# Which engine adds the second convolution tap of the first groups, and which queue stores y of group 3

## The chip, the cores and the metric

The kernel runs on one core of a Trainium2 chip. The metric is the device time of one execution in microseconds (us), as the median of several runs. TensorE is called PE here, VectorE DVE, ScalarE ACT, GpSimd POOL and SyncE SP, as the profile calls them.

## The reference

The input `x` has shape (8, 4224, 192). A causal depthwise convolution with 7 taps comes first: the 192 channels are 8 heads of 24 channels, each head has one softmaxed set of 7 weights, and each output position is the weighted sum of itself and the 6 positions ahead of it. A layer norm and a two-layer MLP (192 to 768 to 192, ReLU) are added to the result.

```python
w = softmax(weight)                       # (8 heads, 7 taps)
y = sum_k w[h, k] * x_padded[s + k]       # per head of 24 channels
xn = (y - mean(y)) / sqrt(var(y) + 1e-6) * g_ln
out = y + relu(xn @ w_ch1) @ w_ch2
```

## The kernel before

**Groups.** Each batch row of 4224 positions is laid on 128 partitions of 33 neighbouring positions. The work is cut into 18 groups of n positions per partition: batch 0 gives groups 0 to 3 with n = 6, 7, 8 and 12, each other batch gives one of 16 and one of 17. In words, a group goes through these steps:

- `load_x(g)` brings x to the tile `xg` (two buffers), issued on SP.
- The convolution makes `y` (two buffers). `first_tap` is 8 ACT multiplies (L336), one per head. `second_tap` is 8 ACT multiplies into a tile `tb` (one buffer, L349), and two DMAs on the POOL queue that add `tb` onto `y` in SBUF (L352); they are called the accumulating DMAs here. `conv(g, k0, k1)` adds taps k0 to k1 - 1 on DVE, 8 instructions per tap (L363).
- `transpose` (L374, DVE) makes `yt` for PE. `store_y` (L431) stores y to the output; later `add_to_out` (L631, POOL queue) adds the MLP's result onto these rows in HBM. `moments` (L389) and `root` are the layer norm's statistics on DVE.
- `up(g)` is the first matrix product on PE (L473); ACT applies the ReLU into `ht` (L485).
- The second product is `down(g)` (L509) for groups 0 to 2, whose results ACT copies out in `park` (L613) and DVE transposes in `finish` (L656). From group 3 on it is `down_fast(g)`: seven half products (`product`, matmuls L553, ACT copies L558) of the Strassen kind, with sums of halves of `ht` on DVE between them (`half_sum`, L531). For group 17 a part of it is done by `down`.

**Order.** The schedule is manual: each engine works through its instructions in the order in which the program issues them, and semaphores do the rest. The loop turns over the groups; in the turn of group g, PE does the products of group g, while DVE finishes the convolution of group g + 1 and ACT starts that of group g + 2. PE has no other work that it could turn to.

In the turn of groups 0 to 2 the taps for g + 2 stand after the ReLUs and ahead of `down`:

```python
conv(g + 1, 2 if g else 1)
transpose(g + 1)
store_y(g + 1)
...
first_tap(g + 2)
second_tap(g + 2)
down(g)
park(g)
```

From group 3 on the 16 tap steps for group g + 2 (8 of `first_tap`, then 8 of `second_tap`) are handed out by `some_taps` in between the half products of `down_fast(g)`; after each of the first four come `many` of them, 3 where n is 16 or 17 and 2 in group 3.

In the turn of group 3 DVE has in order: taps 2 to 4 of group 4, the first three half sums (1,0), taps 5 and 6, the transpose, and inside `down_fast(3)` nine half sum instructions: three for (1,1), three for (0,0), three for (0,1). The fifth half product reads (1,1), the sixth (0,0), the seventh (0,1).

Of the kernel before, what the change touches and what calls it, by code (L numbers as in the profile page):

```python
# [16 lines left out]
def kernel(  # L17
# [27 lines left out]
    nc = tc.nc  # L45
# [10 lines left out]
    J = 17  # L56
# [268 lines left out]
    def first_tap(g, on_act=True, heads=(0, H)):  # L325
        n = groups[g][2]
        if g == 1:

            y[g] = y[0][:, groups[0][2] :]
        elif heads[0] == 0:  # L330
            y[g] = ypool.tile([P, J, D], F32, tag="y", name=f"y{g}")
        for h in range(*heads):
            cs = slice(h * GRP, h * GRP + GRP)
            dst, src, tap = y[g][:, 0:n, cs], xg[g][:, 0:n, cs], taps[:, h, 0:1]
            if on_act:
                nc.scalar.mul(dst, src, tap)  # L336
            else:
                nc.vector.tensor_scalar(out=dst, in0=src, scalar1=tap, scalar2=None, op0=ALU.mult)
# [3 lines left out]
    def second_tap(g, heads=(0, H)):  # L342

        n = groups[g][2]
        if heads[0] == 0:
            tb[g] = bpool.tile([P, J, D], F32, tag="tb", name=f"tb{g}")
        for h in range(*heads):
            cs = slice(h * GRP, h * GRP + GRP)
            nc.scalar.mul(tb[g][:, 0:n, cs], xg[g][:, 1 : 1 + n, cs], taps[:, h, 1:2])  # L349
        if heads[1] == H:  # L350
            for j1, j2 in ((0, n // 2), (n // 2, n)):
                nc.gpsimd.dma_start(  # L352
                    out=y[g][:, j1:j2].rearrange("p j d -> p (j d)"),
                    in_=tb[g][:, j1:j2].rearrange("p j d -> p (j d)"), accum_op=ALU.add,
                )

    def conv(g, k0=1, k1=K, heads=H):
        n = groups[g][2]
        t = xg[g]
        for k in range(k0, k1):  # L360
            for h in range(heads):
                cs = slice(h * GRP, h * GRP + GRP)
                nc.vector.scalar_tensor_tensor(  # L363
                    out=y[g][:, 0:n, cs], in0=t[:, k : k + n, cs], scalar=taps[:, h, k : k + 1],
                    in1=y[g][:, 0:n, cs], op0=ALU.mult, op1=ALU.add,
                )

    def transpose(g):
        n = groups[g][2]
        if g == 1:  # L370
            yt[g] = yt[g - 1][:, groups[0][2] :]
        else:
            yt[g] = tpool.tile([P, J, NC, C], F32, tag="yt", name=f"yt{g}")
        nc.vector.transpose(  # L374
            yt[g][:, 0:n].rearrange("p j c t -> p (j c t)"),
            y[g][:, 0:n].rearrange("p j d -> p (j d)"),
        )
# [3 lines left out]
    def moments(g):  # L381

        n = groups[g][2]
        if g % 2:
            sums[g] = sums[g - 1][:, groups[g - 1][2] :]
        else:
            sums[g] = spool.tile([P, 2 * J, nc.vector.BN_STATS_DIM], F32, tag="st", name=f"st{g}")
        for j in range(n):
            nc.vector.bn_stats(out=sums[g][:, j, :], in_=y[g][:, j, :])  # L389
# [36 lines left out]
        rstd[g] = rt  # L426
        rstd[g + 1] = rt[:, groups[g][2] :]

    def store_y(g):
        b, j0, n = groups[g]  # L430
        nc.sync.dma_start(  # L431
            out=outr[b, :, j0 * D : (j0 + n) * D], in_=y[g][:, 0:n].rearrange("p j d -> p (j d)")
        )

# [93 lines left out]
    def half_sum(g, dst, left, right, op):  # L528
        a = ht[g][0]
        for f in range(FC):  # L530
            nc.vector.tensor_tensor(  # L531
                a[:, *dst, f], a[:, *left, f], a[:, *right, f], op=op
            )

    def down_fast(g):
        n = fast[g]
        w = n * T
        a = ht[g][0]
        cs = cpool.tile([P, NC, NFAST * C], F32, tag="cs", name=f"cs{g}")[:, :, 0 : n * C]
        cs = cs.rearrange("p c (j h t) -> p c j h t", h=2, t=T)  # L540
        part = cpool.tile([P, 3, CH, NFAST * T], F32, tag="part", name=f"part{g}")[:, :, :, 0:w]
        part = part.rearrange("p v c (j t) -> p v c j t", t=T)
        banks = [
            psum.tile([P, 512], F32, tag="ps", name=f"pd{g}_{c}_{i}")
            for c in range(CH) for i in range(2)
        ]

        def product(bank, left, right, to, first):
            for c in range(CH):
                dst = banks[2 * c + bank]  # L550
                for f in range(FC):
                    for q in range(NQ):
                        nc.tensor.matmul(  # L553
                            dst[C * q : C * q + C, 0:w], right[:, f, C * c : C * c + C],
                            left[:, f, q], start=(first and f == 0), stop=(f == FC - 1),
                            skip_group_check=True,
                        )
                nc.scalar.copy(  # L558
                    to[:, c], dst[:, 0:w].rearrange("p (j t) -> p j t", t=T)
                )  # L560

        b = [w2[:, e * FC : e * FC + FC, d * (D // 2) : (d + 1) * (D // 2)]
             for e in range(2) for d in range(2)]
        c11, c21 = cs[:, 0:CH, :, 0], cs[:, 0:CH, :, 1]
        c12, c22 = cs[:, CH:NC, :, 0], cs[:, CH:NC, :, 1]
        todo = [(tap, h) for tap in (first_tap, second_tap) for h in range(H)] if g + 2 < NG else []

        def some_taps(times):
            for tap, h in todo[:times]:
                tap(g + 2, heads=(h, h + 1))  # L570
            del todo[:times]

        many = 3 if n >= J - 1 else 2
        product(0, a[:, 0, 0], b[0], c11, True)
        some_taps(many)
        product(1, a[:, 1, 0], w2sums[:, 2], c22, True)
        some_taps(many)
        product(1, a[:, 1, 1], w2sums[:, 3], part[:, 1], False)
        some_taps(many)
        product(1, a[:, 0, 1], b[2], part[:, 0], True)  # L580
        some_taps(many)
        half_sum(g, (1, 1), (1, 1), (1, 0), ALU.subtract)
        half_sum(g, (0, 0), (1, 1), (0, 0), ALU.add)
        half_sum(g, (0, 1), (0, 1), (1, 1), ALU.subtract)
        nc.vector.tensor_tensor(c11, c11, part[:, 0], op=ALU.add)
        product(0, a[:, 1, 1], w2sums[:, 1], c21, False)
        if g + 1 == NG:
            finish_fast(g, 0, cs, part)
        some_taps(2)
        product(0, a[:, 0, 0], w2sums[:, 0], part[:, 2], False)  # L590
        some_taps(2)
        product(0, a[:, 0, 1], b[3], c12, False)
        some_taps(len(todo))
        return cs, part

    def finish_fast(g, half, cs, part):
        n = fast[g]
        ot = ots[g] if half else out_tile(g)
        fresh = cs[:, CH * half : CH * half + CH, :, 1]
        nc.vector.tensor_tensor(fresh, fresh, part[:, 1 + half], op=ALU.add)  # L600
        for c in range(CH * half, CH * half + CH):
            nc.vector.transpose(  # L602
                ot[:, 0:n, C * c : C * c + C], cs[:, c].rearrange("p j h t -> p j (h t)")
            )
# [73 lines left out]
    for g in range(NG):  # L678
        if g + 2 < NG:
            load_x(g + 2)  # L680
        up(g)
        last = g + 1 == NG
        if not fast[g]:

            conv(g + 1, 2 if g else 1)
            transpose(g + 1)
            store_y(g + 1)
            if g < 2:
                moments(g)
            first_tap(g + 2)  # L690
            second_tap(g + 2)
            down(g)
            park(g)
            if g == 1:
                finish(0)
                root(0)
                w2_sums()
                moments(2)
                finish(1)
            elif g == 2:  # L700
                moments(3)
                root(2)
                finish(2)
            continue
        if not last:
            conv(g + 1, 2, 5)
        half_sum(g, (1, 0), (0, 0), (1, 0), ALU.subtract)
        if not last:
            conv(g + 1, 5, K)
            transpose(g + 1)  # L710
            if g + 2 < NG:
                store_y(g + 1)
        parts = down_fast(g)
        if not last:

            moments(g + 1)
            if g % 2 == 0:
                root(g)
        for half in range(last, 2):
            finish_fast(g, half, *parts)  # L720
        if last:
            add_and_store(g, slice(0, fast[g]))
            down(g)
            finish(g)
# [30 lines left out]
```

## Time and profile before

| | |
|---|---|
| median of 4 runs | 1015.29 us (1014.51 to 1015.6) |
| the profiled execution | 1015.57 us, of which its span is 1013.8 us |
| PE busy | 997.0 us, 98% of the span |
| DVE, ACT, POOL busy | 838.7, 567.3, 64.7 us |
| DMA queue q0 (issued by POOL), q1 (by SP and ACT) | 26.2% and 16.4% of 16 engines' span |
| granted PE clock, mean | 0.998 |

The rows that the prediction reads give the start of a group of instructions in us from the start of the span, then their time, engine, line, operation, output and inputs, shape and count; a bracket at the end holds the idle time ahead of them and what ended it. "issue" in it means that the profile shows nothing that the engine waited for; a wait for a DMA can hide there. Rows of the DMA queues give packets, megabytes and the time of the packets as a share of what 16 engines had in that window.

### The profile page before, as it was taken

How to read it: one execution, taken by the hardware profiler on the slowest of the kernel's cores; microseconds unless marked ns; L12 is line 12 of the kernel's file. 1: busy time of each engine (PE TensorE's matmuls, PEld its weight loads, DVE VectorE, ACT ScalarE, POOL GpSimd, SP SyncE). 2: the span in 40 equal slices, each digit the busy share in tenths (PEclk: the TensorE clock that was granted, in tenths of full speed). 3: DMA queues.
4: the chain of work that ended last, by engine and by line, in shares of the span. 5: the costliest groups of instructions: out<-in, count | busy, mean ns of one | idle time of the engine just before them, and what ended most of it. 6: DMA issues, size and time to landing. Idle time of an engine off the chain costs nothing.

```text
span 1013.8 us, 35726 instructions
## 1 busy us (share of the span) xinstructions
PE 997.0 (98%) x16060; PEld 662.8 (65%) x16060; DVE 838.7 (83%) x1540; ACT 567.3 (56%) x1488; POOL 64.7 (6%) x91
## 2 busy tenths in 40 slices
PE   6999989999999999999999999999999999999997
PEld 5888655568545785458754586556854578545786
DVE  6987896999688997889689896898968799788607
ACT  5738454656546565565646556465654646544451
POOL 1002000000010000000000000000001000000000
PEclk9999999999999999999999999999999999999999
DMA  6256745362537343353732545355253734142031
GB/s 192 92 197 132 206 106 143 63 204 38 177 71 218 66 107 130 75 192 65 205 75 45 188 88 181 67 122 161 38 181 68 219 68 86 52 89 37 2 65 69
DMA packets 16678, 116.14 MB, mean 115 GB/s; under 512 B 2191, under 2 KB 2959, under 8 KB 12430
## 3 DMA queue, kind: packets, MB, share of 16 engines
q0 software_dynamic: 9504, 48.96, 26.2%
q1 hardware_dynamic: 6718, 64.91, 16.4%
q8 instruction: 125, 2.05, 0.8%
q14 instruction: 27, 0.22, 0.1%
q10 hardware_dynamic: 304, 0.00, 0.0%
HBM read 38.95 MB, written 50.23 MB: 88 GB/s over the span
## 4 chain that ended last, share of the span: by engine, by line
PE 84%; DVE 3%; DMA 1%; issue 1%; DVEq 0%
PE ph L473 44%; PE pd L553 39%; DVE y L363 2%; DMA y<-tb 1%; PE po L509 1%; DVE ht L531 1%; DVE y L639 0%; DVE ot L656 0%; DVEq L750 0%; DVE yt L374 0%; DVEq L363 0%; DVEq L531 0%; DVEq L374 0%
## 5 line engine op out<-in xcount | busy, mean ns | idle before, releaser
L473 PE MATMUL ph<-yt,w 32*128 32x256 f32 (+6 forms) x7200 | 517.6, 443 | 0.5 <-DVE yt L374 0.5
L473 PEld LDWEIGHTS ph<-yt,w 32*128 32x128 f32 x7200 | 364.4, 185 | 150.4 <-issue 117.4
L363 DVE SCALAR_TENSOR_TENSOR y<-xg,taps,y 128x408 f32<-128x408 f32 (+5 forms) x724 | 361.1, 581 | 49.3 <-issue 45.4
L485 ACT ACTIVATE ht<-ph 128x256 f32<-128x256 f32 (+6 forms) x600 | 222.7, 458 | 225.9 <-PE ph L473 222.1
L531 DVE TENSOR_TENSOR ht<-ht 128x1024 f32<-128x1024 f32 (+2 forms) x180 | 205.5, 1211 | 102.5 <-PE pd L553 71.7
L553 PE MATMUL pd<-ht,w2sums 128*32 128x256 f32 (+2 forms) x4320 | 238.6, 379 | 3.4 <-DVE ht L531 3.4
L553 PEld LDWEIGHTS pd<-ht,w2sums 128*32 128x32 f32 x4320 | 140.5, 111 | 96.3 <-DVE ht L531 4.6
L553 PE MATMUL pd<-ht,w 128*32 128x256 f32 (+2 forms) x3240 | 182.0, 378 | 0.0
L553 PEld LDWEIGHTS pd<-ht,w 128*32 128x32 f32 x3240 | 103.6, 110 | 74.1 <-issue 8.3
L558 ACT COPY cs<-pd 128x256 f32<-128x256 f32 (+2 forms) x180 | 66.5, 369 | 105.7 <-PE pd L553 105.7
L627 ACT ACTIVATE ot<-ot,r 128x192 f32<-128x192 f32 x247 | 93.1, 471 | 0.0
L558 ACT COPY part<-pd 128x256 f32<-128x256 f32 (+2 forms) x135 | 49.5, 367 | 74.6 <-PE pd L553 74.6
L336 ACT ACTIVATE y<-xg,taps 128x384 f32<-128x384 f32 (+5 forms) x142 | 73.4, 592 | 5.8 <-DVE st L389 5.6
L389 DVE BATCH_NORM_STATS2 st<-y 128x6 f32<-128x192 f32 x264 | 70.2, 354 | 0.0
L349 ACT ACTIVATE tb<-xg,taps 128x408 f32<-128x408 f32 (+3 forms) x128 | 69.7, 603 | 0.0
L631 POOL DMA_DIRECT2D out_dram<-ot x34 | 29.5, 880 | 475.2 <-ACT ot L627 293.9
L602 DVE STREAM_TRANSPOSE ot<-cs 128x512 f32<-128x512 f32 (+2 forms) x90 | 56.6, 679 | 2.2
L374 DVE STREAM_TRANSPOSE yt<-y 128x3072 f32<-128x3072 f32 (+5 forms) x18 | 56.0, 3112 | 2.3 <-ACT w L307 0.5
L352 POOL DMA_DIRECT2D y<-tb x32 | 28.3, 1045 | 435.1 <-ACT cs L558 182.1
L509 PE MATMUL po<-ht,w 128*32 128x192 f32 (+3 forms) x1152 | 51.4, 339 | 0.0
L509 PEld LDWEIGHTS po<-ht,w 128*32 128x32 f32 x1152 | 37.1, 110 | 13.7 <-issue 0.5
L600 DVE TENSOR_TENSOR cs<-cs,part 128x768 f32<-128x768 f32 (+2 forms) x30 | 27.9, 930 | 0.0
(72 smaller groups left out, 147.3 us busy)
## 6 DMA issues: line engine op xcount, KB each, us to landing
y<-tb POOLq DMA_DIRECT2D x21, 768.0 KB, 6.3
xg<-in_x_dram SPq DMA_DIRECT2D x7, 2208.0 KB, 13.1
out_dram<-ot POOLq DMA_DIRECT2D x20, 768.0 KB, 6.6
xg<-in_x_dram SPq DMA_DIRECT2D x7, 2112.0 KB, 13.0
out_dram<-y SPq DMA_DIRECT2D x7, 1536.0 KB, 8.8
out_dram<-y SPq DMA_DIRECT2D x6, 1632.0 KB, 7.8
y<-tb POOLq DMA_DIRECT2D x7, 864.0 KB, 10.0
out_dram<-ot POOLq DMA_DIRECT2D x6, 864.0 KB, 7.3
```

What stands on the lines that cost most here:

```text
L336: nc.scalar.mul(dst, src, tap)
L349: nc.scalar.mul(tb[g][:, 0:n, cs], xg[g][:, 1 : 1 + n, cs], taps[:, h, 1:2])
L363: nc.vector.scalar_tensor_tensor(out=y[g][:, 0:n, cs], in0=t[:, k : k + n, cs], scalar=taps[:, h, k : k + 1], in1=y[g][:, 0:n, cs], op0=AL ...
L389: nc.vector.bn_stats(out=sums[g][:, j, :], in_=y[g][:, j, :])
L473: nc.tensor.matmul(ph[q][:, 0:w], w1[rows, c, fs], t[rows, js, c, :], start=(c == 0), stop=(c == NC - 1),)
L485: nc.scalar.activation(dst, src, AF.Relu)
L509: nc.tensor.matmul(bank[C * q : C * q + C, 0:w], w2[:, f, C * c : C * c + C], t[:, f, q, js.start - fast[g] : js.stop - fast[g], :], start ...
L531: nc.vector.tensor_tensor(a[:, *dst, f], a[:, *left, f], a[:, *right, f], op=op)
L553: nc.tensor.matmul(dst[C * q : C * q + C, 0:w], right[:, f, C * c : C * c + C], left[:, f, q], start=(first and f == 0), stop=(f == FC - 1 ...
L558: nc.scalar.copy(to[:, c], dst[:, 0:w].rearrange("p (j t) -> p j t", t=T))
L602: nc.vector.transpose(ot[:, 0:n, C * c : C * c + C], cs[:, c].rearrange("p j h t -> p j (h t)"))
L627: nc.scalar.mul(ots[g][:, j, :], ots[g][:, j, :], rstd[g][:, j : j + 1])
```

## The change

The convolution's second tap goes to ACT and the accumulating DMA only from group 4 on. For groups 2 and 3 DVE does all of taps 1 to 6, as it did for group 1. In the turn of group 2, `store_y(3)` is issued on the POOL queue, after the two accumulating DMAs of group 4, and no longer on SP ahead of `load_x(5)`. In `down_fast(3)`, `some_taps` hands out 3 tap steps after each of the first four half products where it had been 2.

```diff
-    def store_y(g):
+    def store_y(g, queue=nc.sync):
         b, j0, n = groups[g]
-        nc.sync.dma_start(
+        queue.dma_start(
...
-        many = 3 if n >= J - 1 else 2
         product(0, a[:, 0, 0], b[0], c11, True)
-        some_taps(many)
+        some_taps(3)
         product(1, a[:, 1, 0], w2sums[:, 2], c22, True)
-        some_taps(many)
+        some_taps(3)
         product(1, a[:, 1, 1], w2sums[:, 3], part[:, 1], False)
-        some_taps(many)
+        some_taps(3)
         product(1, a[:, 0, 1], b[2], part[:, 0], True)
-        some_taps(many)
+        some_taps(3)
...
-            conv(g + 1, 2 if g else 1)
+            conv(g + 1)
             transpose(g + 1)
-            store_y(g + 1)
             if g < 2:
+                store_y(g + 1)
                 moments(g)
             first_tap(g + 2)
-            second_tap(g + 2)
+            if g == 2:
+
+                second_tap(g + 2)
+                store_y(g + 1, nc.gpsimd)
             down(g)
             park(g)
```

`conv(g)` without further arguments runs taps 1 to 6. The instructions of PE and their order are the same in both kernels.

## The prediction

> **What bounds the kernel now.** I began with the page, then took the waits of PE, the chain, and the timelines of PE and DVE around the one place that they point to. The page has PE busy for 98% of the span, so only its idle and slow places can give time back. The waits of PE, as total, times and longest, name one that is not in the start-up:
>
> ```profile
> PE idle L313 <- POOL room L251: 4.8, 1, 4.8
> PE pd L553 <- DVE ht L531: 3.4, 3, 2.8
> PE pm L282 <- DVE room L205: 2.7, 1, 2.7
> PE ph L473 <- DVE yt L374: 0.5, 1, 0.5
> ```
>
> The chain that ended last gives the start, length and owner of each piece. It reaches that wait from an accumulating DMA, through DVE's taps of group 4 and its half sums; after 152.41 us it is PE alone until 1007 us.
>
> ```profile
> 106.68 10.54 DMA y<-tb
> ...
> 118.53 3.79 issue
> ...
> 122.43 12.79 DVE y L363 x24
> 135.22 2.61 DVE ht L531 x3
> 137.83 8.48 DVE y L363 x16
> ...
> 152.41 9.85 PE pd L553 x200
> ```
>
> PE's timeline shows the place, the fifth half product of group 3:
>
> ```profile
> 144.79 3.11 PE L553 MATMUL pd<-ht,w 128*32 128x192 f32 x72
> 150.68 0.53 PE L553 MATMUL pd<-ht,w2sums 128*32 128x192 f32 x8 [2.77 <-DVE ht L531]
> 151.55 0.53 PE L553 MATMUL pd<-ht,w2sums 128*32 128x192 f32 x8 [0.34 <-DVE ht L531]
> 152.41 6.93 PE L553 MATMUL pd<-ht,w2sums 128*32 128x192 f32 x128 [0.33 <-DVE ht L531]
> 162.20 31.18 PE L473 MATMUL ph<-yt,w 32*128 32x512 f32 x288
> ```
>
> A half product of 72 instructions takes 3.11 us undisturbed. The fifth could start at 144.79 + 3.11 = 147.90, and three take 9.33 us, to 157.23. `up(4)` starts at 162.20, so this place costs 4.97 us and not just the 3.44 of waits. The rest is in the 128 instructions: at 3.11/72 us each they would take 5.5 us, not 6.93. PE in half-microsecond windows (length, busy time and count, granted clock, DMA share, GB/s) tells why:
>
> ```profile
> 148.50:149.00 0.50, 0.00 (x0) 1.00 0.96 393
> 152.50:153.00 0.50, 0.50 (x8) 0.50 1.03 439
> 156.50:157.00 0.50, 0.50 (x20) 1.00 0.14 33
> ```
>
> The granted clock is 0.5 from about 152.1 to 155.6, some 3.5 us after the long gap, which costs about half of that. DVE's timeline shows why the half sums are late:
>
> ```profile
> 56.72 13.26 DVE L363 SCALAR_TENSOR_TENSOR y<-xg,taps,y 128x192 f32<-128x192 f32 x40 [3.91 <-DMA y<-tb]
> 90.17 17.26 DVE L363 SCALAR_TENSOR_TENSOR y<-xg,taps,y 128x288 f32<-128x288 f32 x40 [6.48 <-issue]
> 122.43 12.79 DVE L363 SCALAR_TENSOR_TENSOR y<-xg,taps,y 128x384 f32<-128x384 f32 x24 [3.90 <-issue]
> 149.70 7.87 DVE L531 TENSOR_TENSOR ht<-ht 128x768 f32<-128x768 f32 x9
> ```
>
> Three times DVE idles ahead of the taps of a group whose second tap comes by DMA (groups 2, 3, 4). From 122.43 to 157.5 it has no gap, so what that last wait gives up, the half sums gain.
>
> **Second tap of groups 2 and 3 on DVE.** Added: 8 instructions at 13.26/40 = 0.33 us (2.65 us) and 8 at 17.26/40 = 0.43 (3.45). Removed: the waits of 3.91 and 6.48. In order: taps of group 2 from 52.8 (end of the moments ahead of them; ACT's first tap ended at 44.7) for 48 x 0.3315 = 15.9, to 68.7 instead of 70.0, so DVE runs 1.3 us early until 83.7, where the transposes of group 1 end; now about 82.4 (the last needs PE's bank of 80.7 and an ACT copy). Taps of group 3: 48 x 0.4315 = 20.7, to 103.1 instead of 107.4. DVE then gets through transpose, moments and root by about 112 and waits for ACT's last copy of `park` (ends 113.1), so it is ready for group 4 at about 113.5, and it was at 118.5. On PE all this lies beside other work: `up(3)` starts at 112.56 and its `yt` is ready at 105.7; without that cover of 6.9 us the price would be the 6.1 us added. ACT loses 16 multiplies (6.4 us), but `second_tap(4)` stands after the ReLUs of `up(2)`, which PE paces: it still ends at 105.8 and its DMAs are issued at 106.1. So DVE's wait for these only grows; their landing decides.
>
> **When they land.** Before, the queues shared the engines; first the window 110.7 to 116.9, then the later accumulating DMAs of group 5, alone, from 166 to 174:
>
> ```profile
> q0 software_dynamic: 123, 0.66, 57.3%
> q1 hardware_dynamic: 128, 1.18, 46.8%
> ```
>
> ```profile
> q0 software_dynamic: 265, 1.62, 100.6%
> ```
>
> The second half of group 4's DMA shared with the store of y (1.18 MB on q1), at half pace. Alone, 1.62 MB took 8 us, so group 4's 1.57 MB takes 7.8. `load_x(6)` alone moved at 397 GB/s, so the 2.26 MB of `load_x(5)` takes 5.7. Now the load is issued first, when the taps of group 3 free its buffer: 103.1, data about 0.7 later (the store issued at 146.3 filled the engines by 147.0), so 103.8. Load and accumulation, in whichever order they interleave, end at 103.8 + 5.7 + 7.8 = 117.3; the store stands behind them in their own queue. Add 1.0 from data to DVE (group 5's: just before 175, DVE at 175.62): 118.3. The mixed traffic of before took 5% more than its parts, some 0.6: 118.9. I take the middle, 118.6, so DVE restarts 3.8 us early; the bounds are 118.0 and 121.6, the latter with the load's data 3.3 us late, as the store of 107.46 was (the engines' q1 packets came after 110.7).
>
> **What that gives on PE.** The three bursts at 150.68, 151.55 and 152.41 follow one half sum each; undisturbed PE would want them at 147.90, 148.25 and 148.60, so they are 2.78, 3.30 and 3.81 us late. 3.8 us early clears all three, with the clock drop; sums (0,0) and (0,1) follow at 0.87 us each ahead of PE's 3.11 per product. DVE cannot use more than about 4.7, since (1,1) overwrites what the third half product reads until 144.8. Gain: 4.97, or 4.9 with a rest of 0.1. At 3.3 early, 0.5 us of waiting would stay; the gain is then 4.5.
>
> **The other two edits.** Three taps per half product: 3 x 0.58 + 3 copies x 0.32 = 2.7 us of ACT in each 3.11 us of PE, so PE's banks come free in time; with ACT 0.4 us slower per product PE would wait that much, four times. It issues the accumulating DMAs of group 5 about 4 us earlier relative to PE. PE does not wait there (DVE idles 8.8 us at 175.6), so nothing. The store on POOL costs one issue of 0.9 us behind which POOL has only `add_to_out(2)`, 127.1. ACT's first tap of group 5 (139.4) must wait for it: it ends near 117.3 + 2.9 + 1.5 = 122. SP now has `load_x(5)` at its head, and nothing else waits.
>
> **Two rules.** The Trainium skill ("TensorE: Matmul & The Clock Gate", section Why this matters for your kernels) has the clock drop after idle gaps of more than about 3 us; here the longest was 2.77, with two of 0.3 behind it, and the clock did drop. By the rule the gain would be the waits alone, 3.4 us; I go by the row. "DMA: Bandwidth & Descriptors", section Issuing engine by pattern, gives plain stores to Sync and speaks against a store from GpSimd; no row here has one.
>
> **The rivals.** (1) The store still gets between the accumulating packets: 2.9 us more, restart at 121.5; DVE gains 0.9 and the clock drop stays: gain about 1, 1014.3. For it: queues share in the rows above. Against: one queue's packets ran in order there, the first half drained before the second. (2) Slower: `load_x(5)`, now in flight when the accumulation starts, slows it more than the store did. It decides once DVE restarts after 122.43; each us beyond costs one. The load took 17.6 us from issue to landing in the mixed traffic; from 103.1 that is 120.7, and if the second half of the accumulation then still needed its own 3.9 us and 1.0 to DVE, DVE would restart at 125.6, 3.2 late: 1018.5. Against: the total work is 2.9 us less and starts 3 us earlier. (3) The waits go but the clock drops all the same, or 0.5 to 1.5 us of waiting remains: gain 2.5 to 4, near 1012.
>
> **Numbers.** The profiled execution took 1015.57, 0.28 over the median; 4.9 off gives 1010.67 and, for the median, 1010.4. Chances: forecast 0.70 (1009.4 to 1011.4), rival (3) 0.14, rival (1) 0.10, rival (2) 0.06. The low end is the full 4.97 with 0.9 for the spread of the runs shown; the high end takes in rival (3). A measurement of this kernel can tell about 0.2%, 2 us: faster 0.84 (forecast and rival (3)), the same 0.10 (rival (1)), slower 0.06 (rival (2)).
>
> **What would show it.** Right: no DVE idle ahead of the taps of groups 2 and 3, `load_x(5)` issued near 103, taps of group 4 starting near 118.6, no wait of PE for L531, `up(4)` near 157.3, no 0.5 clock near 153. Wrong: taps of group 4 starting after 121, or PE waiting for `yt` at `up(3)` or for ACT in group 3.

## The result and the profile after

The changed kernel takes 1013.03 us (median of 35 runs, 1011.63 to 1015.31) beside 1015.06 us for the kernel before on the same chip: a ratio of 0.9982, interval 0.9975 to 0.9989, about 1.8 us faster. 1010.4 was forecast, from 1009.4 to 1011.4, and with rival (3), whose smallest gain was 2.5 us, up to 1012.8. The change does help, by less than half of the forecast. The ratios here and below leave out two executions that were slow as a whole, one of e1 (5245 us) and one of e4 (1315 us). The profiled execution has a span of 1012.0 us.

PE's waits (total, times, longest) still have the entry that the change was to empty:

```profile
PE pd L553 <- DVE ht L531: 2.0, 3, 1.3
```

It has gone from 3.4 to 2.0 us. PE's timeline, start and time first, shows the three late bursts again, in the same place:

```profile
148.65 0.53 PE L553 MATMUL pd<-ht,w2sums 128*32 128x192 f32 x8 [1.34 <-DVE ht L531]
149.52 0.53 PE L553 MATMUL pd<-ht,w2sums 128*32 128x192 f32 x8 [0.34 <-DVE ht L531]
150.39 7.09 PE L553 MATMUL pd<-ht,w2sums 128*32 128x192 f32 x128 [0.34 <-DVE ht L531]
157.29 3.11 PE L553 MATMUL pd<-ht,w 128*32 128x192 f32 x72
160.33 31.18 PE L473 MATMUL ph<-yt,w 32*128 32x512 f32 x288
```

The 128 instructions take 7.09 us, so the half-speed stretch is there too. The windows of PE (length, busy time and count, granted clock, DMA share, GB/s) confirm it:

```profile
148.00:148.50 0.50, 0.00 (x0) 1.00 1.32 369
151.50:152.00 0.50, 0.50 (x12) 0.50 0.69 270
155.50:156.00 0.50, 0.50 (x22) 1.00 0.00 0
```

DVE's timeline shows what became of its three waits:

```profile
52.65 15.88 DVE L363 SCALAR_TENSOR_TENSOR y<-xg,taps,y 128x192 f32<-128x192 f32 x48
82.16 20.65 DVE L363 SCALAR_TENSOR_TENSOR y<-xg,taps,y 128x288 f32<-128x288 f32 x48
120.41 12.79 DVE L363 SCALAR_TENSOR_TENSOR y<-xg,taps,y 128x384 f32<-128x384 f32 x24 [6.49 <-issue]
147.68 7.87 DVE L531 TENSOR_TENSOR ht<-ht 128x768 f32<-128x768 f32 x9
```

The waits ahead of groups 2 and 3 are gone, as the working had it, and the third has grown from 3.90 to 6.49 us. DVE was ready for group 4 at 113.9 and got it at 120.41. The transfers say why. First the window 103.5 to 110.5, then 110.5 to 119 (packets, MB, share of the engines):

```profile
q1 hardware_dynamic: 126, 2.23, 96.6%
```

```profile
q0 software_dynamic: 321, 1.90, 99.7%
q1 hardware_dynamic: 18, 0.04, 1.2%
```

`load_x(5)`, issued on SP at 102.88, has the DMA engines to itself until 110.5. The accumulating DMAs are issued at 105.94 and move nothing until 110.62 (in the profile before the first packet came 1.4 us after the issue). From issue to landing (the first of the two, their median, the second), before and after:

```profile
DMA to landing us min/median/max: 5.7/10.6/15.6
```

```profile
DMA to landing us min/median/max: 10.5/12.1/13.7
```

The first takes longer than before, the second less long. The second is the one that DVE waits for.

### The profile page after: what moved, and what is told of

Read it like the earlier page. It is cut to its first block, busy times and chain, and to the rows that moved or that the text cites. A ratio compares the mean times of both kernels' runs of the same rounds, so it can differ in the third digit from the quotient of the medians.

```text
span 1012.0 us, 35711 instructions
## 1 busy us (share of the span) xinstructions
PE 997.5 (99%) x16060; PEld 663.2 (66%) x16060; DVE 844.7 (83%) x1556; ACT 561.2 (55%) x1472; POOL 62.6 (6%) x88
## 4 chain that ended last, share of the span: by engine, by line
PE 92%; DVE 3%; DMA 2%; ACT 1%; issue 1%; POOL 0%; SPq 0%; DVEq 0%
PE ph L473 49%; PE pd L553 39%; PE po L509 3%; DVE y L363 2%; DMA xg<-in_x_dram 1%; DMA y<-tb 1%; DMA ga<-in_moe_g_ln_dram 1%; DVE ht L531 1%; ACT w L307 0%; ACT tb L349 0%; ACT y L336 0%; PE pc L273 0%; DVE y L638 0%; DVE ot L655 0%; DVE yt L374 0%
## 5 line engine op out<-in xcount | busy, mean ns | idle before, releaser
L363 DVE SCALAR_TENSOR_TENSOR y<-xg,taps,y 128x384 f32<-128x384 f32 (+5 forms) x740 | 367.1, 579 | 36.5 <-issue 36.5
L531 DVE TENSOR_TENSOR ht<-ht 128x1024 f32<-128x1024 f32 (+2 forms) x180 | 205.5, 1212 | 107.5 <-PE pd L553 76.7
L558 ACT COPY cs<-pd 128x256 f32<-128x256 f32 (+2 forms) x180 | 66.4, 369 | 103.5 <-PE pd L553 103.5
L349 ACT ACTIVATE tb<-xg,taps 128x384 f32<-128x384 f32 (+1 forms) x112 | 63.5, 620 | 0.0
L352 POOL DMA_DIRECT2D y<-tb x28 | 24.9, 1049 | 355.4 <-ACT cs L558 177.2
L509 PEld LDWEIGHTS po<-ht,w 128*32 128x32 f32 x1152 | 37.1, 110 | 13.7 <-issue 0.8
```

What stands on the lines that cost most here:

```text
L363: nc.vector.scalar_tensor_tensor(out=y[g][:, 0:n, cs], in0=t[:, k : k + n, cs], scalar=taps[:, h, k : k + 1], in1=y[g][:, 0:n, cs], op0=AL ...
L509: nc.tensor.matmul(bank[C * q : C * q + C, 0:w], w2[:, f, C * c : C * c + C], t[:, f, q, js.start - fast[g] : js.stop - fast[g], :], start ...
L531: nc.vector.tensor_tensor(a[:, *dst, f], a[:, *left, f], a[:, *right, f], op=op)
L558: nc.scalar.copy(to[:, c], dst[:, 0:w].rearrange("p (j t) -> p j t", t=T))
```

## The experiments

Theory A said that the order in which the transfers of this stretch are issued decides when the accumulation of group 4 lands, and that this landing is all that keeps PE waiting. Theory B: the accumulation is late for a reason of its own. Theory C: DVE's half sums are too slow for PE however early they start. The times stand beside runs of the kernel before on the same chip (1014.84, 1015.57 and 1014.84 in the three sets). Two columns of the table come from the profiles and are free of the small offset between executions: how long after `up(3)` began DVE took up group 4, and the time from the start of group 3's first half product to `up(4)`.

| kernel | order of transfers around 103 to 109 | second accumulating DMA, issue to landing | group 4 on DVE after start of `up(3)` | group 3's half products | median, ratio to before (interval) |
|---|---|---|---|---|---|
| before | accumulation, store, load | 15.6 | 9.87 | 26.21 | |
| changed | load, accumulation, store | 13.7 | 8.44 | 24.93 | 1013.03, 0.9982 (0.9975 to 0.9989) |
| e1 | accumulation, store, load | 11.3 | 6.00 | 21.95 | 1011.43, 0.9967 (0.9954 to 0.998) |
| e2 | accumulation, load, store | 16.1 | 10.82 | 26.93 | 1017.58, 1.0023 (1.001 to 1.0036) |
| e3 | store, load, accumulation | 16.1 | 10.78 | 27.66 | 1016.13, 1.0013 (1.0003 to 1.0024) |
| e4 | accumulation, store, load | 11.2 | 5.82 | 21.63 | 1011.95, 0.9968 (0.9957 to 0.9978) |
| e6 | load, store (both on SP), accumulation | 16.5 | 11.25 | 27.90 | 1017.71, 1.0017 (1.0006 to 1.0028) |
| e10 | as e1, and the next pair too | 11.1 | 5.85 | 20.65 | 1009.94, 0.9962 (0.9949 to 0.9975) |

e1, e4 and e10 put all three on one queue; before, store and load stood on the other.

**e1: the load behind.** The changed kernel, with `load_x(5)` taken from SP and queued last on POOL:

```diff
                 store_y(g + 1, nc.gpsimd)
+                load_x(g + 3, nc.gpsimd)
...
-        if g + 2 < NG:
+        if g + 2 < NG and g != 3:
             load_x(g + 2)
```

> The changed kernel, with load_x(5) moved from the head of SP's queue to the POOL queue behind the two accumulating DMAs of group 4 and store_y(3). Theory A (first come, first drained: in the changed kernel load_x(5), issued at 102.9, took the DMA engines until 110.5 and the accumulation, issued at 105.9, only then began to move): the accumulation moves from about 107 to 115, DVE takes up the taps of group 4 at 115.5 to 116.5 instead of 120.4, PE does not wait for L531 at all, up(4) starts near 156.7 instead of 160.3, and the time is 2 us (runs whose clock never drops) to 3.7 us (runs where it drops) below the changed kernel, about 1010. Theory B (the accumulating DMA lands late for a reason of its own, such as POOL's issue or ACT): DVE still starts at about 120.4 and the time stays at 1013. Theory C (DVE's half sums at 0.87 us each are too slow for PE however early they start): DVE starts early, but PE still waits 1 us or more for L531 and the time is 1011.5 to 1013.

B is out: the landing falls from 13.7 to 11.3 us after issue, and the wait for L531 vanishes. C is out with it. DVE restarted later than expected, at 119.27 (in an execution whose PE runs 1.3 us behind that of the changed kernel), but early enough: PE's timeline has no gap at the fifth half product.

```profile
148.43 3.30 PE L553 MATMUL pd<-ht,w2sums 128*32 128x192 f32 x72
152.66 3.13 PE L553 MATMUL pd<-ht,w2sums 128*32 128x192 f32 x72 [0.93 <-ACT cs L558]
155.61 3.11 PE L553 MATMUL pd<-ht,w 128*32 128x192 f32 x72
```

The median is 1011.43 us where about 1010 was expected. A wait of 0.93 us has appeared at the sixth half product; e8 takes it up.

**e2: the store alone.** The kernel before, with `store_y(3)` on the POOL queue behind the accumulation and nothing else changed:

```diff
+            if g < 2:
                 store_y(g + 1)
...
             second_tap(g + 2)
+            if g == 2:
+                store_y(g + 1, nc.gpsimd)
```

> The kernel before with one part of the change: store_y(3) goes to the POOL queue behind the accumulating DMAs of group 4; second taps and tap counts as before. load_x(5) is then issued on SP at about 107.4, after the accumulation (106.1). Theory A: the first half of the accumulation is drained by 111; the second half is either drained too ahead of the load (DVE restarts at 116.5, held to 118.5 by its own work: gain 3.5 to 5 us) or takes turns with the load, 8 packets each per engine at 0.48 and 0.6 us, and ends near 119.8 (DVE restarts at about 121.3, gain about 1 us and up to 1.7 more where the clock does not drop). Theory B: no change from before, 1015.1.

It is slower than before, against the figures of both theories. With the store out of the way `load_x(5)` is at the head of SP and, from 110.6 on, its packets come between those of the accumulation. In the window 110 to 117 the two queues move 81 and 95 packets:

```profile
q1 hardware_dynamic: 95, 1.68, 58.7%
q0 software_dynamic: 81, 0.49, 34.3%
```

DVE's row of group 4:

```profile
123.76 12.79 DVE L363 SCALAR_TENSOR_TENSOR y<-xg,taps,y 128x384 f32<-128x384 f32 x24 [5.03 <-issue]
```

**e3: the taps alone.** The kernel before with all taps of groups 2 and 3 on DVE, the store on SP as it was:

```diff
-            conv(g + 1, 2 if g else 1)
+            conv(g + 1)
...
-            second_tap(g + 2)
+            if g == 2:
+                second_tap(g + 2)
```

> The kernel before with the other part alone: second taps of groups 2 and 3 on DVE; store_y(3) stays on SP ahead of load_x(5). Taps of group 3 end at about 103, and the store (2.9 us of data) and then the load (6.3 us) are in the engines' queues before the accumulation is issued at 106. Theory A: the accumulation moves only from about 113 to 121 and DVE restarts at 122 to 123: no gain against before, 1015 (the 10.4 us of DVE waits that were taken away come back as a longer wait for group 4). Sharing by turns would end the accumulation near 119 to 120 and gain 1 to 2 us. Theory B: restart as in the changed kernel, 120.4, and its time, 1013.

Theory A's figure: DVE takes up group 4 at 123.04 after 8.85 us of waiting. The time is 1.0013 of before, slightly worse than the expected standstill. DVE's earlier end of group 3 only lets the store and the load start ahead of the accumulation.

**e4: the order alone.** The kernel before with its second taps untouched, and store and load both on the POOL queue behind the accumulation:

```diff
+            if g == 2:
+                store_y(g + 1, nc.gpsimd)
+                load_x(g + 3, nc.gpsimd)
```

> The kernel before with its second taps on ACT and by DMA for groups 2 and 3 as they were, and store_y(3) and load_x(5) both on the POOL queue behind the accumulating DMAs of group 4. Theory A: the accumulation lands near 116, DVE is ready for group 4 at 118.5 and starts then, 3.9 us earlier than before; PE's wait for L531 falls from 3.4 to 0.3 us or less, the clock does not drop there, up(4) starts near 157.5 instead of 162.2; gain 3.4 to 4.9 us, about 1010.5, so that the order of the transfers alone would bring more than the whole change did, and the move of the second taps nothing. Theory B: no change from before, 1015.1.

0.9968, the same as e1, at 1011.95 us where about 1010.5 was expected; PE waits 0.8 us at the sixth half product here too. DVE waits no more for group 4 (it starts at 119.34, straight from its own work), and moving the second taps has brought nothing that the order does not bring by itself.

**e5: three taps alone.** `many = 3` in the kernel before.

> The kernel before with the third part of the change alone: three tap steps after each of the first four half products of group 3. Both the prediction and theory A: nothing on PE (ACT has 2.7 us of work per 3.11 us half product); the accumulating DMAs of group 5 are issued near 161 instead of 165.1 and DVE takes up the taps of group 5 about 4 us earlier than 175.6, where PE does not wait for it; PE still waits 3.4 us for L531; time within 0.1% of before. Rival: ACT's later copies hold PE's banks, 0.4 us for each of four half products, and the time rises by up to 1.6 us.

1015.83, ratio 0.9992 (0.9976 to 1.0009): no difference, as expected. Its profiled execution took 1022.23 us, with group 4 on DVE only at 128.54, so it shows how late the accumulation can land in the old order and says little on this edit; it has no wait of PE for ACT's copies.

**e6: the store's queue in the new order.** The changed kernel with `store_y(3)` on SP again, now behind `load_x(5)`.

> The changed kernel with store_y(3) put back on SP, but behind load_x(5). Theory A (in the engines the queues take turns, and a queue's own transfers go in order): the load is moved first as in the changed kernel, then the store's packets take turns with the second half of the accumulation or the first; 2.9 us of store data come ahead of the accumulation's end, DVE takes up group 4 at 122 to 123.3 instead of 120.4, PE's wait grows by about 2 us, and the time is 1015 to 1016. Rival (the store's queue does not matter, as it comes last anyway): 120.4 and 1013.

1017.71, more than expected, and slower than before. On SP the store is issued at 104.34, ahead of the accumulation at 106.90, and not behind it as in the changed kernel; its packets move from 112.1 to 120.4, in turns with those of the accumulation. With the load first, the queue of the store, and with it its place against the accumulation, is worth about 3.5 us (1.0017 less 0.9982).

**e7 and e9: the clock.** The changed kernel with 16, then 6, extra matrix products in PE's gap:

```diff
+        if g == 3:
+            fill = psum.tile([P, 512], F32, tag="ps", name="fill")
+            for _ in range(16):
+                nc.tensor.matmul(fill[0:C, 0:w], w2sums[:, 2, 0, 0:C], a[:, 1, 0, 0, 0], ...)
         product(0, a[:, 1, 1], w2sums[:, 1], c21, False)
```

> The changed kernel with 16 extra matrix products (32 columns by 192, of data at hand, into a bank that nobody reads) on PE ahead of the fifth half product of group 3, about 1.4 us, which fill the idle time of 1.34 us there; DVE and the transfers are as in the changed kernel, so the half sums come as late as before. If the clock drop that follows the gap is due to PE's idle time: no half speed after 150, up(4) starts near 158.9 instead of 160.3 in the profile, and the runs that lost 1.7 us to the drop lose it no more: median 1012 to 1012.4. If the drop has another cause, or is not what makes the runs differ: up(4) at 160.3 and the median stays at 1013.

The 16 products took 5.2 us, far more than the gap of 1.34: median 1015.03, 0.9995 (0.9983 to 1.0006). In the profile the full clock stayed through all of PE's work, though.

> As the version with 16 extra matrix products ahead of the fifth half product of group 3, but with 6: the 16 took 0.163 us each (5.2 us together, as they all go to one set of 32 output columns), far more than the gap; 6 take 1.0 us and end near 148.3, ahead of the first half sum at 148.6. If PE's idle time makes the clock drop: no half speed after 150, up(4) at 158.7 to 159.0 where the changed kernel's profile has 160.3, and the runs of the changed kernel without a drop (about 1012.0) become nearly all. If not: half speed for 3.4 us near 150.5 in the profile and a median of 1013, with the same two groups of times.

Six took 1.95 us, and not 1.0: 0.163 us is the time of one instruction, and each product is two. Half speed did not come behind the gap. e9's windows:

```profile
151.50:152.00 0.50, 0.50 (x16) 1.00 1.26 541
152.50:153.00 0.50, 0.50 (x20) 1.00 0.98 406
```

`up(4)` comes 23.35 us after group 3's first half product instead of 24.93. So this drop follows PE's idle time. The runs agree: 13 of 47 runs of the changed kernel have a mean granted clock of 0.996, which in the profile of e11 stands for two drops, and none of the 23 of e7 and e9. But the runs without any drop did not become nearly all, as was expected: 5 of e9's 11 have 0.998 or less. The profile (0.997) shows where the clock fell instead, in the start-up from 15.0 to 18.5 us:

```profile
16.00:16.50 0.50, 0.50 (x4) 0.50 1.12 395
```

The median was 1013.14, 0.9988 (0.9979 to 0.9997). In the runs at 0.999 or more the products only cost time (median 1012.8, beside 1012.1 for the changed kernel).

**e8: the wait of 0.93 us.** e1, with the next pair, `store_y(4)` and `load_x(6)`, issued by ACT ahead of the last half product instead of by SP at 143:

> The version with load_x(5) behind the store, in which in addition store_y(4) and load_x(6) are issued by ACT ahead of the last half product of group 3 (near 156) instead of by SP at 143. There PE waited no more for half sums, but for 0.9 us at the sixth half product, at 152.66, though the copies and half sums that it needs had ended by 150.8. Theory D: it waited for its own instructions: a 16 KB transfer of the instruction queue was due near 146, behind the packets of store_y(4) and load_x(6), and moved only at 150.3. Then this version has that transfer near 146, no wait there, up(4) at about 156.9 to 157.7 in the profile (0.9 us earlier against the first half product of the group), and a median of 1010 to 1010.6. Rival: the wait is for ACT's copies, as the profile puts it; it stays at 0.9 us and the time at 1011.4.

In e1 the instruction queue's transfer falls into the window 150 to 152, and none into 144 to 150:

```profile
q1 hardware_dynamic: 50, 0.84, 100.3%
q8 instruction: 1, 0.02, 2.9%
```

With the pair out of the way e8 has one in 144 to 146, and PE's 0.93 us are gone (20.61 us for the half products of group 3). The median got worse than e1, 1013.78, 0.9976 (0.9964 to 0.9989), because the pair now stood ahead of the accumulation of group 5. PE's timeline in group 4:

```profile
204.86 0.64 PE L553 MATMUL pd<-ht,w2sums 128*32 128x256 f32 x8 [1.75 <-DVE ht L531]
205.99 0.64 PE L553 MATMUL pd<-ht,w2sums 128*32 128x256 f32 x8 [0.49 <-DVE ht L531]
```

The same error a group later, and one more case for theory A.

**e10: both pairs behind.** e1, with `store_y(4)` and `load_x(6)` on the POOL queue behind the accumulation of group 5:

```diff
         some_taps(2)
+        if g == 3:
+            store_y(g + 1, nc.gpsimd)
+            load_x(g + 3, nc.gpsimd)
         product(0, a[:, 0, 1], b[3], c12, False)
```

> The version with load_x(5) behind the store on the POOL queue, and the same for the next pair: store_y(4) and load_x(6) go to the POOL queue behind the accumulating DMAs of group 5. By theory A and theory D together: DVE takes up group 4 at 117.5 to 119 and PE has no wait at the fifth half product; the instruction transfer moves near 145 and the 0.9 us at the sixth half product are gone (up(4) 20.6 us after the first half product of group 3 begins, where it was 21.95); the accumulation of group 5 is no longer behind the store and the load (issued 155, landed by 165) and PE does not wait in group 4, as it did for 2.7 us when ACT issued that pair ahead of it. Median 1010.0 to 1010.8, 0.5 to 1.3 below the version with load_x(5) alone behind. Rival: some other transfer takes the place of these, and the time is 1011.4 or more.

1009.94 us (median of 5 runs), below both kernels. No half product of group 3 waits:

```profile
147.35 6.08 PE L553 MATMUL pd<-ht,w2sums 128*32 128x192 f32 x144
153.25 3.11 PE L553 MATMUL pd<-ht,w 128*32 128x192 f32 x72
156.28 31.18 PE L473 MATMUL ph<-yt,w 32*128 32x512 f32 x288
```

**e11: the changed kernel again.**

> The changed kernel again, beside the two above on the same chip: a median near 1013, with two groups of times about 1.7 us apart, at a mean granted clock of 0.999 to 1.0 and of 0.998 or less. If the landing of the accumulating DMAs of group 4 scatters from run to run, this profile has DVE taking up group 4 at another time than 120.4, and PE's wait for L531 longer or shorter by as much.

1012.41, 0.9984 (0.9973 to 0.9995). Group 4 on DVE came 8.28 us after `up(3)` began, as in the first profile (8.44), so the landing scattered little here. This profile (mean clock 0.996) has two stretches at half speed, from 15.0 to 18.4 us in the start-up and from 151.5 to 154.9. The runs of the changed kernel, these and the first set, form three groups and not two: near 1012.1 (0.999 and more), 1013.8 (0.997 and 0.998) and 1014.9 (0.996).

## Why the prediction was wrong

**The step that failed is "When they land".** It had DVE restart at 118.6, 3.8 us early. PE runs 0.6 us earlier in the profile after, so 118.0 on its scale; it was 120.41. Taken against PE, DVE was 1.4 us early. The parts: the load's data were to end at 103.2 + 5.7 = 108.9 and ended at 110.5 (they began 0.6 us later, and the window's 2.23 MB in 7.0 us are 319 GB/s where the working took 397); the accumulation then took 8.0 us for 7.8, all but its last few packets; from there to DVE it was 1.9 us for 1.0, as the last packet ended only at 119.87. That is 2.7 us, less the 0.3 by which the middle lay above 118.3. The sum held the order of the two to be of no account, but all of the load stood ahead, so each lateness of the load went straight through. The step treated the load's move to the head of SP as harmless because it starts earlier. e1 shows what it cost: with the load behind, the second accumulating DMA lands 2.4 us sooner after its issue, and DVE takes up group 4 2.4 us sooner after the start of `up(3)` (6.00 for 8.44), which is what was missing. On the scale of before the restart was 121.0, inside the working's own bounds of 118.0 and 121.6; the forecast's range of 1009.4 to 1011.4 still left no room for it.

**The rest of the chain held.** The taps of group 3 were to end at 103.1 (102.5 on the scale of after) and ended at 102.8; DVE was to be ready near 113.5 (112.9) and was at 113.9; the accumulating DMAs were issued at 105.94; the half sums gained exactly what DVE's restart gained (3.44 us of waiting less 1.43 gives 2.01, and 2.0 was measured). ACT with three taps does not hold PE (no wait for its copies in the profile after or in e5's), and the store's landing, 15.9 us after its issue at 107.05, did not hold ACT's first tap of group 5 at 138.81.

**The clock.** The forecast took the loss to half speed, about 1.5 us, as always there. The runs show that it comes and goes, and e9 and e11 that it has a second place, in the start-up, so that a run's mean clock says whether the clock fell and not where. Each profile shows when it fell in group 3: in all seven with a wait of 1.2 us or more at the fifth half product (before, changed twice, e2, e3, e5, e6), in none of the other six. A wait alone does not make it certain: e8's profile has 2.7 us of waits in group 4 and kept the full clock. Of the runs of before in the three sets, 25 of 88 have a mean granted clock of 0.999 or more and a median of 1013.35; of the changed kernel's, 23 of 47, median 1012.12. At full clock the change is worth 1.2 us, near the 1.4 of waiting that went; the rest of the 2 us between the medians is that fewer runs lose clock. The profiled execution after is one of those that do lose it. e10's 1009.94 against 1013.35 is 3.4 us: the waits alone, at full clock.

The Trainium skill's page "TensorE: Matmul & The Clock Gate", section What's actually happening, says that the activity window is about 3.4 us long and runs freely. If so, the same idle time can fall into one window or be split over two, which would fit the groups of runs of one kernel, and the half-speed stretches of 3.4 us in the profiles (6.8 in e3 and e6). Its figure of one idle window for the drop does not fit: 2.0 us of waits, the longest 1.34, were enough in the profile after.

**The rivals.** Rival (2), slower because `load_x(5)` slows the accumulation, had the mechanism right and its size wrong: it did not undo the gain in the changed kernel, but it made e2 (1.0023) slower than before; in e6 (1.0017) the store did its part. Rival (1) was close in its figures, a restart at 121.5 for 121.0 and the drop still there, but not in its reason: the store's packets moved from 118.0 on, when nine tenths of the accumulation were through. Rival (3), 0.5 to 1.5 us of waiting left or the clock drop staying, had the kind right: 2.0 us were left, and in the profile the drop stayed.

**The queue rule.** "DMA: Bandwidth & Descriptors", section Queues, rings and completion order, has each DMA engine take turns between the queues by packets. e2's 81 and 95 packets agree. The changed kernel's trace does not: with the accumulation issued at 105.94, q1 still had the engines to itself until 110.5. In four traces the transfer that came later moved nothing at first: for 2.9 us after its issue the load of e2, for 3.9 the store of before, for 4.7 the accumulation of the changed kernel and for 5.3 that of e3. Then it took turns with what was left of the earlier one, in the changed kernel next to nothing. In e5, whose store was issued only 0.6 us after the accumulation, both moved from 109 on. What sets how long the earlier one keeps the engines stays open.

## What to carry to other kernels

When an edit lets a large transfer start earlier, ask which small transfer on the critical path it now stands ahead of: the two parts of this change were each slower alone (1.0013 and 1.0023) and faster together, and the order of three transfers was worth more than both. Put a transfer that nobody waits for yet behind the urgent one on the same queue, so that it cannot get ahead. Where PE idles for a microsecond or two, look at the granted clock of many runs before a single profile's loss is counted as a gain.

## What was not expected of the hardware

- In e1 PE stood still for 0.93 us up to 152.66 although its inputs were there by 151.8; a transfer of its instruction queue (one packet, 0.02 MB) moved at 150.3, and only after bulk transfers had filled the engines since 144. e4 has the same pair (0.8 us); in e8 and e10, with no bulk transfers in that stretch, both are gone. The profile put the wait down to ACT's copy. That PE waited for its instructions is the reading that fits these four profiles; it was not shown directly.
- Matrix products of 32 columns into one and the same set of 32 output rows took 0.163 us per instruction (e7: 5.20 us for 31 of the 32), where a half product's 72 instructions, spread over four sets, take 3.11 us together, 0.043 each. That those of a half product run side by side is the reading; no run here varies the sets alone.
- One execution of e5 had the accumulation of group 4 late by a further 5.5 us against PE with no edit in that stretch (group 4 on DVE at 128.54). Its store came 0.6 us after the accumulation, where it was 1.3 in the profile before. Single profiles of the old order are not safe to take landings from.
